# wq in place of w3 as the first load of a decode kernel's weight and cache stream, two semaphore steps behind x, with GpSimd's large fills after the cast of x

## The chip, the cores and the metric

One Trainium2 chip, one core. The metric is the device time of one execution in microseconds. A run's record also has the *span*: the time from the first to the last instruction that the profiler recorded. The time is a little longer than the span (the difference: "outside the span").

## The reference

One token for each of 4 sequences. Branch A is attention over a long cache; branch B is a small MLP; the output joins them. Cut to what matters:

```python
B, Sq, D = 4, 1, 448;  Hq, Hkv, Sk, Dh = 16, 8, 8192, 256
# k_cache, v_cache: (4, 8, 8192, 256) bf16, 134 MB each; wq: 448 x 4096; wo: 4096 x 448; w3: 448 x 1792; w4: 1792 x 448
xn = layernorm(x)                                  # 4 x 448
s = attention(xn @ wq, k_cache, v_cache) @ wo      # branch A
x1 = xn + mixed(gelu(layernorm(xn) @ w1)) @ w2     # branch B
g = silu(x1 + gelu(layernorm(x1) @ w3) @ w4)
out = x + s * g
```

Nearly all of the 279 MB read from HBM is the two caches: 32 heads (sequence times KV head) with 4 MB of K and 4 MB of V each. (The kernel doesn't use w1 and w2, before the change or after it.)

## The kernel before

SyncE issues almost every load into one hardware queue, in program order. `ahead` marks instructions that are moved in front of the entry barrier.

```python
def prog_sp(sp):
    ahead.append(sp.dma_start(w3_part_of_vb0, B_w3...).then_inc(S["dw3"], 16))   # 1.6 MB, ahead of the barrier
    sp.dma_start(wq_part_of_vb1, A_wq...).then_inc(S["dwq"], 16)                 # 3.7 MB
    sp.dma_start(w4_sb, B_w4...).then_inc(S["dw4"], 16)                          # 1.6 MB
    def load_k(h):
        if h >= 2:
            sp.wait_ge(S["v_k"], h - 1)          # two K buffers: head h-2 must be transposed
        sp.dma_start(kn_dst(h), A_k_cache[...]).then_inc(...)
    def load_v(h): ...                           # waits v_v, h + 1
    load_k(0); load_k(1)
    load_wo(NLATE, HQ, "dwo")                    # 2.75 MB, 1792 B packets
    for h in range(2, NH):
        load_k(h)                                # the THIRD K load is the first that waits
        load_v(h - 2)
    ...                                          # cut: last V in pieces, rest of wo, store
def take(eng, name, n=1):
    eng.wait_ge(S[name], n).then_inc(S[name], -n)

def prog_act(act):
    ahead.append(act.dma_start(x_sb, x2d).then_inc(S["dx"], 16))                 # x, 3.5 KB
    ...
def prog_pool(gp):                               # memsets, one semaphore count each
    ...                                          # identities, ones_f
    c(gp.memset(pT, 0.0)); c(gp.memset(diag, 0.0)); c(gp.memset(sel, 0.0))
    c(gp.memset(OT, 0.0)); c(gp.memset(po0, 0.0)); c(gp.memset(po1, 0.0)); c(gp.memset(rz, 1.0))

def prog_pe(pe, ...):                            # in order
    # transposes of layernorm(x) and of its second layernorm (VectorE makes them)
    take(pe, "dwq", 16)      ; # 28 matmuls: q = xn @ wq
    take(pe, "dw3", 16)      ; # 49 matmuls with w3
    ...                      ; # transposes of q, matmuls with w4
    for i in range(NWARM):   # NWARM = 14 warm-up matmuls, result unused
        pe.matmul(psv[0:PVW, 0:QW], pT[...], wq_sb[...], start=True, stop=True)
    # loop over heads: transpose K (128 transposes), scores, exp, weighted V
```

VectorE and ScalarE copy K's transposes out of PSUM. After the last of them VectorE raises `v_k`, which frees the K buffer for the load two heads later.

## Time and profile before

| | before |
|---|---|
| time, median of 3 (lowest to highest) | 655.76 us (654.32 to 655.92) |
| the profiled run: time, span | 653.9, 652.1 us |
| load queue's share of 16 DMA engines | 99.5% |
| PE, VectorE, ScalarE busy | 84%, 42%, 39% |

The page of the kernel before, cut to the DMA rows (each digit or number is one of 40 slices) and the queue table (packets, MB, share of 16 engines):

```profile
span 652.1 us, 22853 instructions
...
DMA  9999999999999999999999999999999999999997
GB/s 374 440 418 434 431 432 436 432 432 434 434 426 440 426 442 426 440 428 436 430 434 434 428 440 428 436 430 438 426 440 426 440 428 438 430 434 432 434 429 301
...
q1 hardware_dynamic: 12328, 278.99, 99.5%
```

This reads as a kernel bound by its stream of loads. The first slice (374) holds the start.

The timeline of the first 31 us (start, duration, engine, line, operation; in brackets the idle time before and what ended it; a `q` behind an engine's name means its sequencer, and L271 is the line of `take`):

```profile
0.09 0.41 SPq L215 DMA_DIRECT2D vb<-in_B_w_dram  x1
0.21 0.56 ACTq L324 DMA_DIRECT2D x_sb<-in_A_x_dram  x1
...
1.93 0.36 POOL L293 MEMSET pT<- 128x320 bf16 x1
...
2.36 0.95 POOL L296 MEMSET OT<- 128x1024 bf16 x1
...
3.25 1.00 POOL L298 MEMSET po<- 128x512 f32 x2
3.63 0.89 DVE L397 CAST x_f<-x_sb 4x448 f32<-4x448 bf16 x1 [2.23 <-DMA x_sb<-in_A_x_dram]
...
15.45 3.16 PE L572 MATMUL pst<-vb,xnT 128*8 128x512 bf16 x28 [1.18 <-PEq L271]
...
26.85 4.20 PE L606 MATMUL psv<-vb,pT 128*32 128x512 bf16 x14
...
30.98 1.07 PE L614 MATMUL pst<-ident_b,kn 128*128 128x128 bf16 x16
```

x was issued 0.12 us after w3 but its cast began only at 3.63 us. The q matmuls (line 572) had to wait for wq, which comes behind w3. Then follow 14 warm-up matmuls and, at 30.98 us, head 0. The next view is the timeline of the issuing engine, here the third K load and the first V load:

```profile
42.50 0.33 SPq L230 DMA_DIRECT2D kn<-in_A_k_cache_dram  x1
46.61 0.33 SPq L238 DMA_DIRECT2D vb<-in_A_v_cache_dram  x1
```

### The profile page before, as it was taken

The page shows a single profiled execution, that of the slowest core. Times are in us where ns is not written, and L with a number is a line of the kernel's source. Part 1 is how long each engine was busy: PE and PEld are TensorE (multiplying, and loading weights), DVE is VectorE, ACT ScalarE, POOL GpSimd, SP SyncE. Part 2 cuts the span into 40 slices and gives each one's busy share as a digit, 9 for nine tenths or more (in the row PEclk, how much of TensorE's full clock was granted, in tenths as well). Part 3 has the DMA queues.
Part 4 walks back from the last instruction along what each step waited for, and adds up shares of the span by engine and source line. Part 5 has one row for each costly group of instructions (what it writes and reads, how often), then busy time and mean ns, then how long its engine had stood idle before and what let it go on. Part 6 is the DMA issues. An engine that isn't in the chain of part 4 may idle for free. (4 is left out here: it accounts for less than half of the span.)

```text
span 652.1 us, 22853 instructions
## 1 busy us (share of the span) xinstructions
PE 550.6 (84%) x9937; PEld 471.0 (72%) x9937; DVE 274.9 (42%) x589; ACT 255.8 (39%) x364; POOL 13.4 (2%) x77
## 2 busy tenths in 40 slices
PE   0898997987887988878898888997888898888898
PEld 0486886976776887657687766777776698767685
DVE  7353554343443444434433443443344344334442
ACT  4154454442343443324443333444343344333340
POOL 2000000000000000000000000000000000000000
PEclk9799999797799878989977889897789988878989
DMA  9999999999999999999999999999999999999997
GB/s 374 440 418 434 431 432 436 432 432 434 434 426 440 426 442 426 440 428 436 430 434 434 428 440 428 436 430 438 426 440 426 440 428 438 430 434 432 434 429 301
DMA packets 12353, 279.13 MB, mean 428 GB/s; under 512 B 1204, under 2 KB 3256, under 8 KB 3768
## 3 DMA queue, kind: packets, MB, share of 16 engines
q1 hardware_dynamic: 12328, 278.99, 99.5%
q8 instruction: 7, 0.11, 0.1%
q10 hardware_dynamic: 16, 0.01, 0.0%
q14 instruction: 2, 0.02, 0.0%
HBM read 278.99 MB, written 0.00 MB: 428 GB/s over the span
## 5 line engine op out<-in xcount | busy, mean ns | idle before, releaser
L614 PE MATMUL pst<-ident_b,kn 128*128 128x128 bf16 x4096 | 343.6, 237 | 77.8 <-PEq L271 76.2
L321 ACT ACTIVATE kT<-pst 128x1024 bf16<-128x1024 bf16 x224 | 229.3, 1024 | 356.1 <-ACTq L271 355.0
L614 PEld LDWEIGHTS pst<-ident_b,kn 128*128 128x128 bf16 x4096 | 272.0, 107 | 83.4 <-issue 82.8
L319 DVE COPY kT<-pst 128x1024 bf16<-128x1024 bf16 x288 | 197.5, 691 | 256.7 <-DVEq L271 256.7
L626 PE MATMUL psc<-qc,kT 128*128 128x2 bf16 x4096 | 178.4, 164 | 0.0
L626 PEld LDWEIGHTS psc<-qc,kT 128*128 128x128 bf16 x4096 | 157.4, 98 | 28.3 <-issue 28.1
L665 PE MATMUL psv<-vb,pT 128*4 128x512 bf16 x1056 | 87.4, 382 | 1.7 <-issue 1.7
L644 PE MATMUL psm<-sel,po 128*128 128x2 f32 x272 | 36.8, 257 | 0.5 <-PEq L271 0.5
L644 PEld LDWEIGHTS psm<-sel,po 128*128 128x128 f32 x272 | 34.7, 196 | 1.0 <-issue 1.0
L665 PEld LDWEIGHTS psv<-vb,pT 128*4 128x4 bf16 x1056 | 22.4, 82 | 17.2 <-issue 3.0
L478 DVE TENSOR_REDUCE rmax<-psc 128x2 f32<-128x128 f32 x32 | 9.3, 292 | 50.2 <-DVEq L271 50.2
L496 DVE COPY po<-psv 128x512 f32<-128x512 f32 x34 | 23.5, 692 | 3.0 <-DVEq L271 2.3
L483 DVE TENSOR_REDUCE gmax<-psm 2x1 f32<-2x128 f32 x32 | 8.9, 279 | 35.8 <-DVEq L271 35.8
L343 ACT ACTIVATE pT<-psc,negb 128x64 bf16<-128x64 f32 x66 | 20.6, 332 | 5.4 <-ACTq L271 5.4
L306 POOL COPY qc<-qT 128x4 bf16<-128x4 bf16 x32 | 5.9, 186 | 584.0 <-DVEq L495 565.3
L638 PEld LDWEIGHTS psm<-diag,ones_f 2*128 2x128 f32 x66 | 13.3, 250 | 6.4 <-issue 5.2
L638 PE MATMUL psm<-diag,ones_f 2*128 2x2 f32 x66 | 16.1, 310 | 1.1 <-PEq L271 0.9
L343 ACT ACTIVATION_READ_ACCUMULATOR pT<-psc,negb 128x1 f32 x66 | 13.6, 206 | 0.0
L634 PEld LDWEIGHTS psm<-ident_f,rmax 128*2 128x2 f32 x32 | 2.6, 80 | 14.4 <-issue 14.4
L562 PE MATMUL pst<-ident_b,xn_b 4*128 4x4 bf16 x14 | 0.6, 161 | 13.6 <-DVE xn_b L391 8.9
L656 PE MATMUL psm<-rowsum,ones_f 128*128 128x2 f32 x64 | 11.6, 251 | 0.0
L562 PEld LDWEIGHTS pst<-ident_b,xn_b 4*128 4x128 bf16 x14 | 0.5, 99 | 13.7 <-issue 8.9
(101 smaller groups left out, 117.8 us busy)
## 6 DMA issues: line engine op xcount, KB each, us to landing
kn<-in_A_k_cache_dram SPq DMA_DIRECT2D x32, 4096.0 KB, 24.9
vb<-in_A_v_cache_dram SPq DMA_DIRECT2D x31, 4096.0 KB, 30.4
vb<-in_A_wq_dram SPq DMA_DIRECT2D x1, 3584.0 KB, 14.6
vb<-in_B_w_dram SPq DMA_DIRECT2D x2, 1568.0 KB, 12.4
wo_sb<-in_A_wo_dram SPq DMA_DIRECT2D x1, 2688.0 KB, 43.7
kn<-in_A_v_cache_dram SPq DMA_DIRECT2D x1, 2048.0 KB, 25.9
kn<-in_A_v_cache_dram SPq DMA_DIRECT2D x1, 1024.0 KB, 27.9
kn<-in_A_v_cache_dram SPq DMA_DIRECT2D x2, 512.0 KB, 29.0
```

Source lines behind the costliest of these rows:

```text
L319: engine.tensor_copy(dst, src).then_inc(S["v_ev"], 1)
L321: engine.activation(dst, src, ACT.Copy).then_inc(S["a_ev"], 1)
L343: ins = act.activation(pv_p[:, :, hh], sc[:, :, hh], ACT.Exp, bias=negb[:, s, hh:hh + 1], scale=SCALE, accum_out=rowsum[:, s, hh:hh + 1])
L478: v.tensor_reduce(rmax[:, :], psc[h % 2][:, 0:NCH * REP].rearrange("p (k h) -> p h k", h=REP), AX.X, ALU.max).then_inc(S["v_rmax"], 1)
L483: v.tensor_reduce(gmax[:, :], psm[0:REP, 0:P], AX.X, ALU.max).then_inc(S["v_s"], 1)
L496: v.tensor_copy(po[:, slot], psv[:, 0:CP * DH]).then_inc(S["v_po"], 1)
L614: ins = pe.transpose(dst[:, t * P:(t + 1) * P], kn[:, h % 2, GC * j + kl, half * P:(half + 1) * P], ident_b[:, :])
L626: ins = pe.matmul(psc[h % 2][:, kk * REP:(kk + 1) * REP], kT[:, j % RING, t * P:(t + 1) * P], qc[:, h % 2, half, :], start=(half == 0), st ...
L638: pe.matmul(psm[:, P:P + REP], ones_f[0:REP, :], diag[:, :], start=True, stop=True).then_inc(S["p_m2"], 1)
L644: ins = pe.matmul(dst(dh)[:, 0:width], po[:, slot, i * DH + dh:(i + 1) * DH:NHALF], sel[:, i, 0:width], start=(i == 0), stop=(i == CP - 1))
L656: pe.matmul(psm[:, P + REP:P + 2 * REP], ones_f[:, :], rowsum[:, h % 2, :], start=True, stop=True)
L665: ins = pe.matmul(psv[o:o + CP * REP, 0:CP * DH], pT[:, h % 2, kk * REP:(kk + CP) * REP], src[:, kk:kk + CP, :].rearrange("p c d -> p (c d)"),
```

## The change

Intent: x should arrive before the stream fills the DMA engines (in the packet records of before, x's first packet moved at 2.37 us, 1.26 us after w3's first), wq should come first because q is needed first, and GpSimd's large fills should not run beside VectorE's cast of x (0.89 us there). The rest of PE's prologue should move forward with them. The diff, cut to its core:

```diff
-    for load in loads:
+    for load in reversed(loads):
@@
         def prog_sp(sp):
+            ahead.append(sp.sem_inc(S["pause"], 1))
+            ahead.append(take(sp, "pause"))
             ahead.append(sp.dma_start(
-                vflat[0][:, 0:DK * FH], B_w3...).then_inc(S["dw3"], 16))
-            sp.dma_start(vflat[1][:, 0:DK * HDH], A_wq...).then_inc(S["dwq"], 16)
+                vflat[1][:, 0:DK * HDH], A_wq...).then_inc(S["dwq"], 16))
+            sp.dma_start(vflat[0][:, 0:DK * FH], B_w3...).then_inc(S["dw3"], 16)
@@
         def take(eng, name, n=1):
-            eng.wait_ge(S[name], n).then_inc(S[name], -n)
+            return eng.wait_ge(S[name], n).then_inc(S[name], -n)
@@
             c(gp.memset(ones_f[:, :], 1.0))
-            c(gp.memset(pT..., 0.0))
             c(gp.memset(diag[:, :], 0.0))
             c(gp.memset(sel..., 0.0))
-            c(gp.memset(OT..., 0.0))
+            c(gp.memset(rz..., 1.0))
+            gp.wait_ge(S["v_c"], 2)          # the cast of x is done
+            c(gp.memset(pT..., 0.0))
             for i in range(2):
                 c(gp.memset(po[:, i], 0.0))
-            c(gp.memset(rz..., 1.0))
+            c(gp.memset(OT..., 0.0))
```

(`reversed` only keeps the order of the three instructions that are moved ahead of the barrier.)

More of the change, by code (lines that the diff above doesn't have):

```diff
@@ L181, in bass_recurrent_scan__gqa_block_cached__mixer_s_mlp__decode_kernel @@
         S = {n: es.enter_context(nc.semaphore(n)) for n in (
-            ["dx", "dwq", "dw3", "dw4", "dwo", "dk0", "dk1", "dv0", "dv1", "dout"]
+            ["dx", "dwq", "dw3", "dw4", "dwo", "dk0", "dk1", "dv0", "dv1", "dout", "pause"]
             + ["dvl%d" % i for i in range(NPIECE)] + ["dwl%d" % i for i in range(len(LATE))]
@@ L214, in prog_sp @@
         def prog_sp(sp):
+            ahead.append(sp.sem_inc(S["pause"], 1))
+            ahead.append(take(sp, "pause"))
             ahead.append(sp.dma_start(
-                vflat[0][:, 0:DK * FH],
-                B_w3.rearrange("d (t n) -> (d t) n", t=NHF).rearrange(
-                    "(p j) n -> p (j n)", j=DK)).then_inc(S["dw3"], 16))
-            sp.dma_start(vflat[1][:, 0:DK * HDH],
-                         A_wq.rearrange("d (t n) -> (d t) n", t=NHF).rearrange(
-                             "(p j) n -> p (j n)", j=DK)).then_inc(S["dwq"], 16)
+                vflat[1][:, 0:DK * HDH],
+                A_wq.rearrange("d (t n) -> (d t) n", t=NHF).rearrange(
+                    "(p j) n -> p (j n)", j=DK)).then_inc(S["dwq"], 16))
+            sp.dma_start(vflat[0][:, 0:DK * FH],
+                         B_w3.rearrange("d (t n) -> (d t) n", t=NHF).rearrange(
+                             "(p j) n -> p (j n)", j=DK)).then_inc(S["dw3"], 16)
             sp.dma_start(w4_sb.rearrange("p a k n -> p a (k n)"),
@@ L292, in prog_pool @@
             c(gp.memset(ones_f[:, :], 1.0))
-            c(gp.memset(pT[:, :, :].rearrange("p s n -> p (s n)"), 0.0))
             c(gp.memset(diag[:, :], 0.0))
             c(gp.memset(sel[:, :, :].rearrange("p c n -> p (c n)"), 0.0))
-            c(gp.memset(OT[:].rearrange("p g r d b -> p (g r d b)"), 0.0))
+            c(gp.memset(rz[:, :, :].rearrange("p s r -> p (s r)"), 1.0))
+            gp.wait_ge(S["v_c"], 2)
+            c(gp.memset(pT[:, :, :].rearrange("p s n -> p (s n)"), 0.0))
             for i in range(2):
                 c(gp.memset(po[:, i], 0.0))
-            c(gp.memset(rz[:, :, :].rearrange("p s r -> p (s r)"), 1.0))
+            c(gp.memset(OT[:].rearrange("p g r d b -> p (g r d b)"), 0.0))
             assert c.n == NPC
```

## The prediction

> **What bounds the kernel now.** The page's DMA row stands at 9 tenths in all but the last of 40 slices; the queue table gives the load queue 99.5% of 16 engines' span. [...] steady slices here show 426 to 442[...]. The DMA records show the first w3 packet at 1.1 us and the last v_cache packet landing at 643.9 us: 279 MB in 642.8 us is 434 GB/s. About 8 us of tail follow, from the last landings to the store. So time = start of the stream + bytes at 434 GB/s + tail, as long as the queue never runs dry.
>
> It doesn't: in the timeline of the issuing engine the third K load is issued at 42.5 us, while wo moves until 46.3; later loads are issued 5 to 10 us before the queue would empty.
>
> **What the change moves.** (1) The first load waits for two semaphore steps on its own engine. Estimate from a like round trip in the timeline (GpSimd memset ending at 1.07, its dependent starting at 1.31): 0.2 us later. This is on the critical path. (2) x goes ahead of the stream. Before, it was issued at 0.21 us, its packets started at 2.4 us, behind w3's, and its cast began at 3.63. I expect 2.4. (3) GpSimd's pT, po and OT fills (0.36 + 1.00 + 0.95 us) move behind the cast, which took 0.89 us beside the po fill; a tensor_scalar of the same 4x448 took 0.50. Alone I expect 0.4 to 0.6. [...] The fills should end by 6.5 us, before ScalarE's fill of the vb rest (10.6 before, about 9 after). (4) wq lands at about 10.5 us (3.67 MB at 434 GB/s from 1.4, plus completion) in place of 15.2. Before, the q matmuls waited from 14.2 to 15.4 for it; after, they wait for LayerNorm and start at about 13. w3 lands about 14, before its matmuls at 16. PE's prologue ends 2 to 2.5 us earlier; the transposes of head 0 start near 29 us in place of 30.98, then held by K0's landing.
>
> **How much is critical.** None of (2) to (4): they issue no load into an empty queue, PE is busy 84%, and from head 1 on it waits for K. The third K load will be issued near 40.5 us and queue longer. What is left is (1), +0.2 us, with the start-up of a stream of 28 KB rather than 12.5 KB packets unknown by some 0.3 us either way.
>
> **Prediction:** 655.8 us, 8 times in 10 between 654.2 and 657.2 (the runs before spread over 1.6 us). Faster by over 2%: 0.01; within 2%: 0.98; slower: 0.01.
>
> **What would show each step.** First packet at 1.3 to 1.5 us, x's before it; cast at 2.2 to 2.7 us, near 0.5 us long; pT fill right after; q matmuls at 12.5 to 13.5 us; head 0 near 29 us; third K load 1.5 to 2.5 us earlier; last v_cache landing within 0.5 us of 643.9; tail unchanged.
>
> **What would make it wrong.** The stream's end depending on PE after all, so that 2 us come off; semaphore steps costing over 1 us; the larger packets starting slower or faster; GpSimd's late fills holding LayerNorm.

The sum had one term left, +0.2 us for (1), on three times before of 654.32 to 655.92 us, and came to 655.8.

## The result, and the profile after

| | before | after |
|---|---|---|
| median of 6 runs (lowest to highest) | 655.54 us (654.32 to 655.94) | 653.53 us (653.39 to 655.72) |
| ratio, 95% interval | | 0.9979, 0.9964 to 0.9995 |
| span of the profiled run | 652.06 us | 652.08 us |

Ratios are the mean time of one kernel's runs over that of the other's runs of the same rounds, so they are not quite the ratio of the medians. All outputs are right. The change is a small but clear gain of 0.2%. It lies within 2%, as was said, but the median lies below the predicted range (654.2 to 657.2).

The two profiled spans are equal. Who compares only these two traces finds no gain at all. The spans of all runs say more: 44 runs of the kernel before, timed beside the experiments, and 11 of the kernel after (6 of this result, 5 of a later repeat):

| | runs | time, median | span, mean | span, median | spans of 653.0 or more | outside the span, median |
|---|---|---|---|---|---|---|
| before | 44 | 654.97 us | 653.22 us | 653.10 us | 28 | 1.85 us |
| after | 11 | 653.54 us | 652.44 us | 652.10 us | 2 | 1.44 us |

So there are two separate gains: 0.8 us in the mean span (1.0 in the median), and 0.41 us outside it. And the profiled run of the kernel before was a lucky one: only 8 of its 44 spans are 652.5 us or less.

The page of the kernel after, cut in the same way, is the same picture:

```profile
span 652.1 us, 22855 instructions
...
DMA  9999999999999999999999999999999999999997
GB/s 375 441 416 440 425 440 428 438 428 436 432 424 444 422 446 420 446 422 444 424 440 428 440 426 440 424 440 428 430 438 426 442 424 444 424 442 426 440 425 299
...
q1 hardware_dynamic: 12328, 278.99, 99.5%
```

The timeline after, with the lines that answer to those of before:

```profile
0.21 0.56 ACTq L327 DMA_DIRECT2D x_sb<-in_A_x_dram  x1
0.24 0.41 SPq L217 DMA_DIRECT2D vb<-in_A_wq_dram  x1
...
1.63 0.61 DVE L400 CAST x_f<-x_sb 4x448 f32<-4x448 bf16 x1 [0.23 <-DMA x_sb<-in_A_x_dram]
...
2.30 0.36 POOL L299 MEMSET pT<- 128x320 bf16 x1
2.60 0.99 POOL L301 MEMSET po<- 128x512 f32 x2
...
3.52 0.96 POOL L302 MEMSET OT<- 128x1024 bf16 x1
...
11.91 3.16 PE L575 MATMUL pst<-vb,xnT 128*8 128x512 bf16 x28
...
23.82 5.68 PE L609 MATMUL psv<-vb,pT 128*32 128x512 bf16 x14
...
29.92 1.05 PE L617 MATMUL pst<-ident_b,kn 128*128 128x128 bf16 x16 [0.42 <-PEq L273]
```

The cast of x begins 2.0 us earlier, the q matmuls 3.5 us earlier, the warm-ups 3.0 us earlier, and head 0 only 1.06 us earlier. Where 2 us went on the way is in the next view: busy times of PE, weight loads, VectorE, ScalarE and GpSimd in three stretches, then the granted PE clock, the DMA share and GB/s. First the kernel before:

```profile
22.00:25.00 3.00, 1.34 (x14) 0.41 (x14) 1.29 (x8) 0.25 (x1) 0.31 (x2) 0.51 1.00 426
25.00:29.00 4.00, 3.19 (x12) 1.18 (x11) 1.66 (x4) 0.39 (x1) 0.00 (x0) 0.51 0.97 418
29.00:31.00 2.00, 2.00 (x11) 0.74 (x10) 0.00 (x0) 0.00 (x0) 0.00 (x0) 1.00 1.07 451
```

And the kernel after:

```profile
22.00:25.00 3.00, 2.19 (x9) 0.80 (x8) 1.01 (x3) 0.39 (x1) 0.00 (x0) 0.50 0.91 393
25.00:29.00 4.00, 4.00 (x11) 1.41 (x10) 0.65 (x2) 0.00 (x0) 0.00 (x0) 0.52 1.01 430
29.00:31.00 2.00, 1.58 (x20) 1.01 (x18) 0.32 (x1) 0.00 (x0) 0.00 (x0) 1.00 0.99 426
```

In both runs the granted clock came back to 1.00 at 28.9 us. The earlier warm-ups simply ran longer at half clock (5.68 against 4.20 us; in both traces they follow each other by 0.43 us at half clock and by 0.21 to 0.22 at full), and PE then stood idle for 0.42 us. The clock alone did not set head 0: in e10, e12 and e13 below, the warm-ups end earlier (28.4 to 29.2 us in place of 29.5), and head 0 still begins at 29.95 to 30.09 us (more under "What stays open"). In the traces the clock records have values 0.5 and 1.0 alone, and each but the last of a trace lasts a multiple of 3.41 us (at half clock 3.4, 6.8 or 10.2 us, and once 17.1 in e5). In the profiles of the kernel before and of the experiments without the whole change (e1, e2, e3, e6, e9, e11, e14 below) the return to full clock falls between 28.4 and 31.2 us. Where it came at 30 us or later with 14 warm-ups (e1, e3, e11), head 0 began at 31.5 to 32.0 us in place of 31.0.

The third K load and the first V load after:

```profile
41.62 0.33 SPq L232 DMA_DIRECT2D kn<-in_A_k_cache_dram  x1
45.73 0.33 SPq L240 DMA_DIRECT2D vb<-in_A_v_cache_dram  x1
```

The third K load is issued 0.88 us earlier. To see what this is worth, the DMA packet records were read. Each load ends with a small completion write (4 bytes) on each of the 16 DMA engines, and the first and the last of the 16 tell when the fastest and the slowest engine finished:

| us from the span's start | before | after |
|---|---|---|
| first packet of the stream | 1.11 | 1.26 |
| wo finished, fastest / slowest engine | 43.94 / 46.31 | 44.12 / 45.88 |
| third K load issued | 42.50 | 41.62 |
| its packets can start (issue + 1.03) | 43.53 | 42.65 |
| **margin** to the fastest engine | **+0.41** | **+1.47** |
| last v_cache packet landed | 646.7 | 646.7 |

The 1.03 us are measured at the start of the stream: issue at 0.09, first packet at 1.11, and 0.24 to 1.26 after. (0.6 us of it follow the 0.41 us of the issue itself. In the five profiles below whose margin is under -0.6 us, the third K load's first packet follows its issue by 0.95 to 0.97 us.) The prediction compared the issue at 42.5 us with the end of wo on the *slowest* engine, 46.3 us, and called the queue full. The fastest engine was done at 43.9, and with the latency only 0.4 us were left, in a run whose clock came back earlier than in e1, e3 and e11.

### The profile page after: what moved, and what is told of

Read it like the earlier page. It is cut to its first block, busy times and chain, and to the rows that moved or that the text cites. A ratio compares the mean times of both kernels' runs of the same rounds, so it can differ in the third digit from the quotient of the medians.

```text
span 652.1 us, 22855 instructions
## 1 busy us (share of the span) xinstructions
PE 553.9 (85%) x9937; PEld 473.0 (73%) x9937; DVE 274.7 (42%) x589; ACT 256.3 (39%) x364; POOL 13.7 (2%) x77
## 5 line engine op out<-in xcount | busy, mean ns | idle before, releaser
L659 PEld LDWEIGHTS psm<-rowsum,ones_f 128*128 128x128 f32 x64 | 9.5, 188 | 0.0
```

Source lines behind the costliest of these rows:

```text
L659: pe.matmul(psm[:, P + REP:P + 2 * REP], ones_f[:, :], rowsum[:, h % 2, :], start=True, stop=True)
```

## The experiments

Theories. A: the gain comes from a cleaner start of the stream. B: the gain comes from an earlier issue of the third K load, which in most runs of the kernel before meets DMA engines that have already run dry. C: the end is set by the slowest DMA engine, and which one that is depends on where the program's own instruction fetches (0.88 to 0.96 us each for PE's in the trace of before) fall; the rest is chance. The kernel before ran beside each group (11 runs each).

### The parts alone: e1, e2, e3

e1 has only the two steps (with `reversed`); e2 only the order of w3 and wq; e3 only GpSimd's part. Each is the hunk of that part in the diff above.

> The kernel before with the two semaphore steps alone: x ahead of the stream, w3 still the first load, GpSimd as before. Theory A (start of the stream: what matters is that x's small packets are out of the way and the first packets start cleanly): the whole gain, ratio about 0.997 to 0.998. Theory B (an earlier prologue of PE issues the third K load earlier, before the fastest DMA engines run dry): PE still waits for wq until about 15.4 us, so no gain, ratio 0.9995 to 1.0005, third K load near 42.5 us. Theory C (the end is set by the slowest of the 16 DMA engines, and which engine that is depends on where the instruction fetches of about 1 us fall, which differs from run to run): single runs scatter between 653.4 and 656 us here as in every variant, and the profiled time goes with the largest lag of an engine behind the fastest (2.2 us at a profiled 653.9 us).

> wq in place of w3 as first load, issued at once as w3 was; no pause, GpSimd as before. x's packets now queue behind 28 KB packets, so x lands later than the 3.3 us of before, about 3.5 to 4.5 us, and the q matmuls start at 14 to 15 us. Theory A: no gain or a loss, ratio 0.9995 to 1.002. Theory B: the gain in part, PE's prologue 1 us earlier, ratio near 0.999. Theory C: as for e1, scatter from 653.4 to 656 us.

> GpSimd's large fills behind the cast alone, loads as before. The cast (0.89 us beside the fills) should take 0.6 us and the LayerNorm chain end 0.3 us earlier, but q still waits for wq at 15.4 us. Theories A and B: ratio 0.9995 to 1.0005. Theory C: scatter from 653.4 to 656 us.

| | median | ratio to before, 95% | spans, mean (range) | outside | margin in the profile |
|---|---|---|---|---|---|
| e1 steps | 655.45 | 1.0000, 0.9985 to 1.0016 | 653.68 (652.3 to 654.3) | 1.47 | -0.95 |
| e2 order | 654.72 | 0.9994, 0.9980 to 1.0008 | 652.70 (651.9 to 653.4) | 1.87 | +0.91 |
| e3 GpSimd | 654.76 | 0.9994, 0.9979 to 1.0009 | 652.92 (652.8 to 653.2) | 1.86 | -0.92 |

No part alone has a clear gain. Theory A falls with e1: the same clean start as after (x's packets first, first packet of the stream at 1.26 us), and no gain. But the profiles of e1 and e3 caught what the profile of before had missed. The issuing engine's timeline in e1:

```profile
43.94 0.33 SPq L232 DMA_DIRECT2D kn<-in_A_k_cache_dram  x1
```

By then the fastest engine had 0.08 us of work left. The bytes moved from 44 to 50 us (last number: GB/s) show the hole. The kernel before (profiled in a lucky run):

```profile
44.00:50.00 6.00, 5.50 (x100) 4.27 (x99) 3.19 (x8) 2.14 (x4) 0.19 (x1) 1.00 1.06 449
```

The kernel after:

```profile
44.00:50.00 6.00, 4.95 (x94) 4.10 (x87) 3.18 (x8) 2.47 (x6) 0.19 (x1) 1.00 1.09 462
```

e1:

```profile
44.00:50.00 6.00, 5.95 (x104) 4.01 (x101) 3.24 (x8) 1.32 (x2) 0.19 (x1) 1.00 1.02 387
```

(A packet's bytes are counted where it starts, so short stretches can exceed the true rate; the comparison between kernels is what counts.) In e1's packet records, between 44.5 and 45.0 us only 6 to 7 of 16 engines are busy. The third K load's first packets, of 32 KB, then take 1.6 to 2.4 us in place of 1.21; the reason was not tested. e1 and e3 also differ in where the cast stood: 0.92 us beside the large fills, 0.38 us alone (e2, e3), 0.61 us beside the small ones (after).

### PE late or early on purpose: e4, e5, e6, e7

Only the number of warm-up matmuls is changed:

```diff
-    NWARM = 14
+    NWARM = 20   # e4, on the kernel after;  40: e5, on after;  8: e6, on before;  8: e7, on after
```

> The changed kernel with 6 more warm-up matmuls of 512 columns (14 to 20), so that PE starts head 0 some 1.3 to 2.6 us later than in the changed kernel, as late as in the kernel before or later; the third K load is issued near 43 us. Theory A: the gain stays, ratio to before 0.997 to 0.998. Theory B: the gain is lost, ratio 0.9995 to 1.003. Theory C: scatter from 653.4 to 656 us, no steady difference from the changed kernel, since the slowest engine has 2.8 us to spare at the third K load.

> The changed kernel with 40 warm-up matmuls in place of 14, so that PE starts head 0 late on purpose: at full clock they take 0.21 us each, so head 0 starts near 33 to 35 us and the third K load is issued at 45 to 47 us, 2 to 4 us after the fastest DMA engines have finished wo. Theory B (a load issued into an empty queue): the span grows by 2 to 3.5 us over the changed kernel's 652.1 and all runs lie above 655 us; the trace shows the first packet of that load 1.0 us after its issue, with engines idle before it. Theories A and C: no change, 653.4 to 654.3 us.

> The kernel before with 8 warm-up matmuls in place of 14 and nothing else, so that PE starts head 0 some 1.2 us earlier (29.7 us in place of 31 to 32). Theory B: the third K load is issued before 42.5 us and the span falls to about 652.1 to 652.8 us, time 653.9 to 654.6 us, ratio 0.998 to 0.999: the gain in span without the change. The part of the time outside the span stays at 1.85 us, as in every kernel without the pause (1.44 us with it). Theories A and C: as before, 654 to 656.6 us.

> The changed kernel with 8 warm-up matmuls. Theory B: the third K load is issued at 40 to 41.5 us; the margin, already positive, grows, so the best time stays near 653.4 us, but the slower runs (654.3 and 655.7 of six) should go: all runs 653.3 to 654.0. If the warm-up is needed for the clock, head 0 runs longer at half clock and the margin is lost again. Theories A and C: as the changed kernel, with its scatter.

| | median | ratio to before | spans, mean (range) | head 0 or issue | margin |
|---|---|---|---|---|---|
| e4 | 654.22 | 0.9983 | 652.64 (652.2 to 652.9) | head 0 at 29.58 | +1.05 |
| e5 | 660.46 | 1.0080 | 659.02 (657.7 to 660.8) | issue at 45.66 | -2.64 |
| e6 | 654.41 | 0.9991, 0.9979 to 1.0003 | 652.58 (651.7 to 653.3) | issue at 42.26 | +0.51 |
| e7 | 654.97 | 0.9997 | 653.52 (653.2 to 653.9) | issue at 43.38 | -0.31 |

e4 missed its aim. Its profiled run got full clock at 26.5 us, so PE was no later, and it tells nothing between the theories. e5 is a clear dose: the queue ran quite empty (no engine busy from 45.75 to 46.5 us), and the fastest engine needed 12.92 us for the third K load in place of 9.68. The total rose more than expected, though, by 6.6 us: the longer program also shifted its instruction fetches (17 for PE in place of 7), and in the middle of the run another load came 1.8 us late (its stage took 12.01 us in place of 9.68). e6 gave the expected earlier issue and mean span in the kernel *before*, but the interval of its ratio includes 1. e7 took the second branch of its expectation. After its few warm-ups PE stood idle for 2.9 us, and the clock fell back to half just as head 0 began (column before the last two: 0.52), which made the third K load late; the spans of all its runs fit that:

```profile
30.00:33.50 3.50, 3.25 (x28) 3.07 (x29) 0.69 (x1) 1.02 (x1) 0.00 (x0) 0.52 1.02 440
```

### An earlier signal that was none: e9, e10

```diff
         def evac(engine, h, j):
             take(engine, "p_td" if j in D_GROUPS else "p_ta")
+            if j == NGR - 1:
+                engine.sem_inc(S["v_k"], 1)
@@
-                    v.sem_inc(S["v_k"], 1)
                     f_rmax(h)
```

e9 is this on the kernel before, e10 on the kernel after.

> The kernel before with one thing moved: the signal that a K buffer is free is given when the last transposes of a head are done, ahead of VectorE's copy of them (0.69 us) in place of after it. Neither the prologue nor the start of the stream changes. Theory B: the third K load is issued about 0.7 us earlier, so its margin is mostly positive; spans 652.0 to 653.0 in place of 652.1 to 654.8, mean 0.5 to 0.8 us lower; part outside the span still 1.85 us; time 653.9 to 654.8. Theories A and C: spans as before, mean 653.3.

> The changed kernel with the same early signal: margin of the third K load about 2 us. Theory B: no run with a dry queue is left, spans 651.8 to 652.8, time 653.3 to 654.2, as the best runs of the changed kernel and without its 655.7. Theory C: scatter like that of the changed kernel (spans 651.9 to 654.3).

The issue did not come earlier. In e9:

```profile
42.90 0.33 SPq L230 DMA_DIRECT2D kn<-in_A_k_cache_dram  x1
```

In e10 it came at 42.00 us. The premise was wrong, and the trace of before had shown it. VectorE's last two copies of head 0 there:

```profile
41.79 1.34 DVE L319 COPY kT<-pst 128x1024 bf16<-128x1024 bf16 x2 [0.47 <-DVEq L271]
```

They end at 43.13 us, but the K load was issued at 42.50. So the bare semaphore increment, which stands behind the copy in VectorE's program, took effect at least 0.63 us before the copy ended. In before, after, e9 and e10 alike the issue comes 0.2 us after PE's last transposes of the head end, with the edit or without it. Spans: e9 652.1 to 654.4, mean 653.00; e10 652.2 to 653.1, mean 652.64; ratios 0.9998 and 0.9983. They are repeats of before and after, no more.

### The third K load alone: e13

This is the kernel after with one issue delayed and PE left as it is:

```diff
                 if h >= 2:
                     sp.wait_ge(S["v_k"], h - 1)
+                for _ in range(16 if h == 2 else 0):
+                    sp.sem_inc(S["pause"], 1)
+                    take(sp, "pause")
                 sp.dma_start(kn_dst(h), ...)
```

> The changed kernel with 16 pairs of semaphore steps on the issuing engine between the wait that frees the K buffer and the issue of the third K load alone; a pair took 0.15 us, so that one issue comes some 2.5 us later and nothing else moves (PE, clock and prologue stay). Theory B: the load's packets come 2.5 us later, margin about -1.2 us, the fastest engine needs 11.3 to 11.8 us from the end of wo to the end of that load in place of 9.68, and the span rises by 1.2 to 1.8 us to about 653.5 to 654.2; the part outside the span stays at 1.44. If the dry queue is only a companion of a late PE and not the cause, the span stays at 651.9 to 652.8.

Median 655.04 us, ratio to before 1.0001 (0.9988 to 1.0014). The spans are 652.9 to 653.9, mean 653.48: 1.0 us above the kernel after, a little under the expected 1.2 to 1.8. Head 0 started at 29.97 us, as after (29.92). The cast of x came at 2.54 us in this profile, 0.9 later than after, which moved the q matmuls (12.59 us) but not head 0. The issue:

```profile
43.93 0.33 SPq L235 DMA_DIRECT2D kn<-in_A_k_cache_dram  x1
```

and the bytes from 44 to 50 us:

```profile
44.00:50.00 6.00, 5.95 (x116) 4.96 (x109) 3.66 (x9) 3.34 (x7) 0.19 (x1) 1.00 1.03 398
```

So the late issue itself costs the time, not something else that goes along with a late PE. In this trace the loss stands at that one load: every later stage took 9.68 us but one (9.91, at 384 us, where the longer program's instruction fetch now falls), and the last landing of the stream came at 649.94 us in place of 648.93. All profiles together, sorted by margin (the stage is the fastest engine's time from the end of wo to the end of the third K load):

```
kernel          margin us   stage us
e5 warm-up 40     -2.64      12.92
e1 steps only     -0.95      11.28
e3 GpSimd only    -0.92      11.15
e13 late issue    -0.91      11.09
e11 (below)       -0.62      10.95
e7 after, 8       -0.31      10.52
e9                +0.02      10.17
before            +0.41       9.85
e6 before, 8      +0.51       9.87
e2, e14           +0.91, +0.93   9.69, 9.70
after and its variants (e4, e8, e10, e12, e15)  +1.05 to +1.49   9.68 to 9.69
```

Below a margin of about 0.5 to 0.7 us the stage grows by about 0.5 to 0.7 us less the margin; above it, it stays within 0.02 us of 9.68. Those 0.5 us or more are of the size of the slow first packets (0.4 to 1.2 us over 1.21 in e1); which of the two makes the other is not shown.

The margin does not explain all of a span. From the last landing to the end of the span, eight profiles take 3.1 us (before, after, e2, e3, e6, e9, e12, e14), the nine others 3.5 to 4.0 us. In the nine, PE was late and not the loads: its last 24 matmuls follow the ones before at once, while in the kernel after they first wait 0.31 us, by the program's order for the late pieces of wo. All nine had 6.8 us at half clock that began about 36 us before the end of the span; the eight had only 3.4 us of it in the last 50 us, or none. So 0.3 to 0.9 us of the scatter go with where the half-clock stretches fall at the end. The last landings, which are free of this, sort by margin more clearly than spans do: 648.6 to 649.2 us in all profiles with a positive margin, 649.6 to 650.3 us below -0.3, and 655.6 us in e5.

### The time outside the span: e8, e11

e8 is the kernel after with the two steps doubled. e11 is the kernel before with the same two steps in a harmless place:

```diff
             load_wo(NLATE, HQ, "dwo")
+            sp.sem_inc(S["pause"], 1)
+            take(sp, "pause")
```

> The changed kernel with four semaphore steps in place of two ahead of the first load. The stream starts 0.15 us later again (first packet at 1.4 us), so the span grows by 0.15 us at most. If the 0.41 us that the runs with the pause spend less outside the span is a constant of having any semaphore step ahead of the first load, it stays at 1.44 us and the time is 653.5 to 653.7; if it goes with the number of steps, it falls to about 1.0 us.

> The kernel before with the same two semaphore steps put after the initial loads, where the issuing engine waits anyway: the start of the stream is untouched, only the program of that engine is two instructions longer. If the 0.41 us outside the span come from where the end of that program falls (in the traces an 8 KB instruction fetch lies 1.1 us after the end of the span in kernels without the steps and at its end in those with them), the part outside the span falls from 1.85 to 1.44 us here too. If they come from the start (x or a semaphore step ahead of the first load), it stays at 1.85. Spans as before, 652.1 to 654.8 us.

e8: median 653.88 us, ratio 0.9980 (0.9968 to 0.9992), spans 652.1 to 653.0, outside 1.41 us. e11: median 654.19, ratio 0.9983 (0.9971 to 0.9995), spans 652.0 to 653.6 (mean 652.72), **outside 1.44 us**, with w3 still first at 0.09 us and x still behind it. So the 0.41 us have nothing to do with x or the order: two more instructions in the issuing engine's program bring them, wherever they stand, and four bring no more. What goes along with it is an 8,192-byte instruction fetch. The last of these starts 1.1 to 1.4 us after the end of the span in the kernels without the two extra instructions (before, e2, e3, e6, e9, e14), and within 0.1 us of its end in the kernel after, e1, e4, e5, e7, e10, e11, e12 and e15; with still longer programs of the issuing engine it lies far earlier (e8 at 621.6 us, e13 at 384.3 us). That the position of this fetch at the end of the program is the mechanism is argued from this, not shown. Two cautions. The ratio of e11, which is padding alone, is nearly that of the whole change (0.9983 against 0.9980 for e12 in the same rounds): its mean span, too, was 0.5 us below the kernel before's, which six runs with this scatter don't settle. And the nine profiles with the longer end of the span all have the two steps or more, while none of the six without them does; if that is not chance, such runs give the 0.41 us back inside the span. Both profiles of the changed kernel (after, e12) have the short end.

### The parts together: e12, e14, e15

e12 is the kernel after again; e14 is the kernel after without the two steps (and without `reversed`); e15 is the kernel after with GpSimd's part undone.

> The changed kernel itself again, beside the others on one chip: span 651.9 to 652.8 in most runs with one in six near 654, part outside the span 1.44 us, median 653.5 to 654.0, ratio 0.998.

> The changed kernel without the two semaphore steps (wq first and GpSimd's fills moved, as in the change). Part outside the span back at 1.85 us; spans 652 to 653.4, mean 652.6, as with the order alone; time 653.8 to 655.2, so 0.4 to 0.9 us above the changed kernel.

> The changed kernel with GpSimd's fills left where they were (wq first and the two steps, as in the change). If GpSimd's part does nothing for the time: spans as in the changed kernel (651.9 to 652.8 in most runs), part outside the span 1.44 us, median 653.5 to 654.0. If it carries part of the gain through a shorter LayerNorm chain: cast of x 0.9 us in place of 0.61, third K load issued 0.3 us or more later, mean span 652.8 or more.

| | median | ratio to before, 95% | spans, mean (range) | outside |
|---|---|---|---|---|
| e12 after | 653.60 | 0.9980, 0.9967 to 0.9993 | 652.32 (651.9 to 653.1) | 1.45 |
| e14 no steps | 655.30 | 1.0011, 0.9995 to 1.0027 | 653.42 (651.9 to 655.0) | 1.88 |
| e15 no GpSimd part | 654.35 | 0.9992, 0.9978 to 1.0006 | 652.80 (652.0 to 653.7) | 1.45 |

Without the steps the gain is gone, more than expected. x then stands behind 28 KB packets of wq, its cast starts at 4.99 us, and the q matmuls at 15.03 us, hardly earlier than before. The order and the steps together move q: each alone leaves q waiting, for x in e14 and for wq in e1 (q at 15.53 us); together q starts at 11.9 to 12.2 us (after, e15). But this does not explain e14's time: its profiled run, the fastest of the six, issued the third K load at 42.05 us with a margin of +0.93, as e2 did, and yet two of its other runs have spans of 654.4 and 655.0 us. Those left no trace, so what slowed them is open, and e14 does not speak for theory B. GpSimd's part shortened the cast (0.91 us in e15, 0.61 after). Whether it moves the time can't be told: 652.80 against 652.44 us of mean span, with a scatter of 0.7 us from run to run.

No version faster than the changed kernel came out of this.

## Why the prediction was wrong

- **The step that failed:** "It doesn't: in the timeline of the issuing engine the third K load is issued at 42.5 us, while wo moves until 46.3", and from it "None of (2) to (4): they issue no load into an empty queue". The 16 DMA engines finish wo 2.4 us apart. The fastest was dry at 43.9 us, and a load needs 1.03 us from issue to first packet. The profiled run had a margin of 0.4 us where 0.5 us are needed. With a later clock (e1, e3, e11: issue at 43.55 to 43.94) it was negative, and the stage took 1.3 to 1.6 us longer. e13 showed that this wait, put back alone, takes the gain in the span away. That most runs of the kernel before had it is inferred: only one of them was traced, and of the four other profiles whose q matmuls start as late, with 14 warm-ups (e1, e3, e9, e11), three had a negative margin and one +0.02.
- **"What is left is (1), +0.2 us":** the stream did start 0.15 us later (1.11 to 1.26 us). But the sum lacked two terms, each larger: about -0.8 us of mean span, from (4) as far as e13 and the margins tell, and -0.41 us outside the span, which depends on the length of the issuing engine's program and was not in the prediction at all.
- **One profile was taken for the kernel.** The profiled run of before, 653.9 us, was below all three timed ones (654.32 to 655.92). That was on view, and said that the profile showed a better case than the median.
- **A misreading:** "the last v_cache packet landing at 643.9" is not in the trace: it landed at 646.7 us, and wo's last piece at 648.9. The tail is 3 us after the last landing, not 8. The conclusion did not rest on it; the rate is 431, not 434 GB/s.
- **(2)** right in kind, under-sized: the cast started at 1.63 us, not 2.4, because x's packets (1.17 us) were quite alone. **(3)** right: 0.61 us, at the upper edge of the predicted 0.4 to 0.6, and 0.38 us alone (e2, e3). With nothing, small fills and large fills of GpSimd beside it the cast took 0.38 (e2, e3), 0.61 (after) and 0.89 to 0.92 us (before, e1, e15); what makes it slower beside them was not shown. **(4)** q started at 11.9 us, earlier than the predicted 13, and did not wait for wq, as predicted. But head 0 came at 29.92 us, 0.9 us later than predicted, though the warm-ups, at half clock until 28.9 us, are only part of the reason: where they ended earlier (e10, e12, e13), head 0 came no earlier (see what stays open).
- **The tail** was unchanged in the two profiles, as predicted (the store landed 0.52 us before the end of the span in both), and "within 2%" held. In other profiles it was up to 0.9 us longer (see e13).

What stays open: the single slow run of the kernel after (655.72 us), whose trace was not kept; the two slowest runs of e14; and whether head 0, for which PE waited 0.3 to 2.9 us in the kernel after and six variants, waits there for K (its last completion at 28.7 us in after) or for its own instructions (a 16 KB fetch that ends at 28.7 us). The traces point to the instructions: in all seven profiles head 0 starts 1.22 us after that fetch ends, against 1.16 to 1.24 us after K's last completion, and the q matmuls of the kernel before started 0.46 us after the last completion of wq. Theory C is not the cause of the gain; of the scatter that remains, a part goes with the clock at the end of the run, and a part may be of C's kind.

## What to carry to other kernels

Here the queue was as full as its *first* engine to run dry (43.94 us in the kernel before, the last at 46.31): compare the issue of the next load, plus the latency from issue to first packet (about 1 us here, and 0.5 us or more of room on top), with the earliest of the 16 completions, not with the last. Before reading a profile as the kernel, see where its time stands among the timed runs; where the spread is as large as the effect, one trace shows one case of it. And split a small gain into span and rest: 0.41 us here came with two instructions of padding that had nothing to do with the intent.

## What else the traces measured

- Each 16 KB instruction fetch of PE took 0.88 to 0.96 us (seven in the kernel before), and in this stream, at 426 to 442 GB/s in 37 of 40 slices, a lag between engines was not made up: in the kernel before the distances between the 16 completions of a load stay the same to about 0.02 us from 83 to 325 us, and after the seven fetches and the uneven start the slowest engine ended 2.2 us behind the fastest.
- A dry queue cost more than the gap itself: 32 KB packets took 1.6 to 2.4 us at the restart (e1) in place of 1.21, and the stage 1.60 us longer at a margin of -0.95. The 16 engines of the load queue were 2.4 us apart before and 1.8 us after by the end of wo, still 2.2 and 2.0 us in the last K load.
- Transposes did not end full clock in this mix: in the kernel before the granted clock, once it had come back during the warm-ups, stood at 1.0 from 28.9 to 63.0 us, a stretch in which PE did 256 transposes (8 in 0.61 us), 256 two-column matmuls and some 55 of 512 columns. No run has transposes alone.
